# A three-phase float32 chain on one core: weight loads and splits moved between slots, a transposition done earlier, the third phase's first slot in another order

## The chip, the cores and the metric

One core of one Trainium2 chip runs the whole kernel. The metric is the device time of one execution in microseconds; before the change it was 1579.04 (median of 3 runs, 1578.59 to 1579.18).

## The reference

Inputs are float32, with batch 8, 8 heads, sequence 576, head size 64, so 4608 tokens of 512 features.

```python
kv = einsum('bhsd,bhse->bhde', k, v)
o  = einsum('bhsd,bhde->bhse', q, kv)
x  = o / sqrt(mean(o * o, -1) + 1e-6) * g_norm      # -> [4608, 512]
h  = x @ w_in                                        # [4608, 2048]
g  = (a0 + a1 h + a2 h^2 + a3 h^3) / (1 + |b0| |h| + |b1| h^2 + 1e-6)
x2 = g @ w_out                                       # [4608, 512]
e  = (x2 @ w1) * (x2 @ w2)                           # [4608, 1024]
out = (e @ w3) @ w_out2                              # [4608, 512]
```

The kernel gets the weights as float64 and makes float32 of them.

## The kernel before

Every product is made of three float32r matmuls: an operand is split into a rounded part `hi` (ScalarE) and the rest `lo` (VectorE), and `hi*hi`, `hi*lo` and `lo*hi` are summed in PSUM. The program is in manual order: each engine runs its instructions in the order in which the Python code issues them, and all transfers are issued by SyncE (SP) in that order. A tile is known by its tag; a new tile of a tag waits until the readers of the tile that it replaces are done. The names in the trace are those of the tiles.

**First phase** (to about 975 us): attention and the first pair of layers. Float64 weights are converted on the way.

**Second phase** (about 970 to 1332 us): `x2 @ w1` and `x2 @ w2`, combined in a seven-product scheme of Strassen's kind. `c_slot(n)` runs 48 times (6 groups of columns, `j`, times 8 feature blocks, `i`), and once more to drain; a slot holds seven products of six 128x384 matmuls each. In slot n TensorE does `a` and `c` of n, then `c` of n-1, `d` of n, `d` of n-1, and `b` and `a` of n. VectorE starts a slot by adding the carried sums to slot n-1's banks (L800 to L803), and products `c` and `d` of n-1 wait for that. Other work hangs on the slots in two lists: `extra1[n]` runs after the first two products, `extra2[n]` after slot n-1's `d`. The weights' pieces come in four sets of two feature blocks (`cw_load`, `cw_work`, the closures numbered 0 to 10); sets 0 and 1 are made on the boundary of the phases, set 2 in slots 2 and 3 and set 3 in slots 4 and 5, in runs of three or four closures. Slot 6 to 8 of each group make the next group's pieces of x (`gen_work`). `w_out2` (8 tiles, into the places `wa0` to `wa7`) is loaded in slots 44 and 45 (L882) and split in slots 46 and 47, four tiles at a time (`split_in`, L643 and L645). In slot 47 the first row of `w3` is loaded (`w3_load`, L866).

**Between the phases** the product `w3 @ w_out2` is built row block by row block, in the order `ROWS` = 0, 4, 1, 5, 2, 6, 3, 7. `w3_turn` transposes one row block of `w3` on TensorE (8 transposes, L874) and splits the result (L84, L85); the first turn stands ahead of the draining slot 48. `w_row(n)` does 24 matmuls 128x512 (L88 to L90) into one bank, and after its fifth k-step it turns the next row block. A row block lies in two tiles (tags `xh` and `xl`, two buffers each); the load for row n+2 is issued after row n. `w_out_row(n)` copies the bank out (L915) and makes the pieces `wq` of the third phase's weights. After each row two closures of `first_e` run: the sums and splits of the first 256 tokens of `e`.

**Third phase** (from 1387.81 us): `d_slot(n)`, 18 times and once to drain, again seven products, of twelve 128x256 matmuls each (L991), with the same waits between slots. `e_load(n)` loads 256 tokens of `e` in two halves of 512 KB into the tags that `R_SLOT` names (L952); for n = 1 the second half's tag is `wa7`, which holds a tile of `w_out2` until the last row is done. `e_work(n+1)`'s sums and splits run inside `d_slot(n)`: the lists `gen[0]` to `gen[2]`, two sums ahead of the first splits and two more between them.

Of the kernel before, what the change touches and what calls it, by code (L numbers as in the profile page):

```python
# [8 lines left out]
F32 = mybir.dt.float32  # L9
# [9 lines left out]
def linear_attention_two_moe_kernel(  # L19
# [24 lines left out]
    nc = tc.nc  # L44
# [362 lines left out]
    with tc.manual_schedule():  # L407
# [386 lines left out]
        def c_slot(n):  # L794
            cur = n if n < NGC else None
            e = cg.get(n - 1)
            if e:
                j_, i_ = divmod(n - 1, KF2)
                w_, q_ = cw[i_ // IP], pieces
                nc.vector.tensor_tensor(out=e["c"], in0=e["c"], in1=e["u"], op=ALU.add)  # L800
                e["c22"] = st_tile("c22")
                nc.vector.tensor_tensor(out=e["c22"], in0=e["c"], in1=e["p5"], op=ALU.add)
                nc.vector.tensor_tensor(out=e["d"], in0=e["d"], in1=e["u"], op=ALU.add)  # L803
                aS = st_tile("c11")
                nc.scalar.copy(aS, e["a"])
            if cur is not None:
                j, i = divmod(n, KF2)
                w, q = cw[i // IP], pieces
                f = cg[n] = {}
                names = ("at", "h", "h", "kv") if n % 2 == 0 else ("acc0", "acc1", "acc2", "acc3")  # L810
                for x, tag in zip("abcd", names):
                    f[x] = ps_tile(tag, [P, TA], 2 if tag == "h" else 1)
                prod(f["a"], w[A11], i, q[j, B11], True)
                nc.scalar.copy(f["b"], f["a"])
                prod(f["c"], w[S3], i, q[j, T3], True)
            for work in extra1.get(n, ()):
                work()
            if e:
                prod(e["c"], w_[A22], i_, q_[j_, T4], False)
                eo = wp.tile([P, 2, TA], F32, tag="wb15", name="eo")  # L820
                nc.vector.tensor_tensor(out=eo[:, 0, :], in0=aS, in1=e["c"], op=ALU.mult)
            if cur is not None:
                prod(f["d"], w[S1], i, q[j, T1], True)
                f["p5"] = st_tile("p5")
                nc.scalar.copy(f["p5"], f["d"])  # L825
            if e:
                prod(e["d"], w_[S4], i_, q_[j_, B22], False)
            for work in extra2.get(n, ()):
                work()
            if e:  # L830
                nc.vector.tensor_tensor(out=eo[:, 1, :], in0=e["c22"], in1=e["d"], op=ALU.mult)
                nc.sync.dma_start(
                    out=ed[i_, :, j_ * 2 * TA:(j_ + 1) * 2 * TA], in_=eo.rearrange("p a b -> p (a b)")
                )
                del cg[n - 1]
            if cur is not None:
                prod(f["b"], w[S2], i, q[j, T2], False)
                prod(f["a"], w[A12], i, q[j, B21], False)
                f["u"] = st_tile("u")
                nc.scalar.copy(f["u"], f["b"])  # L840

# [18 lines left out]

        def w3_load(i):
            for c in range(2):
                e = xp.tile([P, 3, W], F32R, tag=f"x{'hl'[c]}", name="w3")
                nc.sync.dma_start(out=f32(e[:, 2, :]), in_=w3d[i, :, c * W:(c + 1) * W])  # L866
                w3t[i, c] = e

        def w3_turn(i):
            for c in range(2):  # L870
                e = w3t[i, c]
                pt = ps_tile(("at", "kv")[c], [P, 4, P])
                for j in range(4):
                    nc.tensor.transpose(pt[:, j, :], f32(e[:, 2, j * P:(j + 1) * P]), ident)  # L874
                split(pt.rearrange("p j f -> p (j f)"), e[:, 0, :], e[:, 1, :])

        wo2 = {}
        wc = {}
# [7 lines left out]
        def w_row(n):  # L886
            i = ROWS[n]
            acc = ps_tile("h", [P, DM], bufs=2)
            for j in range(KF2):
                e = w3t[i, j // 4]  # L890
                sl = slice(j % 4 * P, (j % 4 + 1) * P)
                mm3(acc, e[:, 0, sl], e[:, 1, sl], *wo2[j], j == 0, j == KF2 - 1)
                if j == KF2 - 4 and n + 1 < KF2:
                    w3_turn(ROWS[n + 1])
            return acc

        NQ = DM // 2
        NPD = NT // (2 * P)  # L900
        KH = KF2 // 2
        wq = {}

        def wq_new(m):
# [7 lines left out]
        def w_out_row(n, acc):  # L912
            c, hf = n // 2, n % 2
            r = stp.tile([P, DM], F32, tag="st", name="wr")
            nc.scalar.copy(r, acc)  # L915
            wrow[hf] = r[:, :NQ], r[:, NQ:]

            def to(m, t):
                if m not in wq:
                    wq_new(m)  # L920
                split(t, *wq[m][c])

            if hf == 0:
                b11, b12 = wrow[0]
                to(B11, b11)
                sub(b11, b12, b11)
                to(T1, b11)
                return
            t1, b12 = wrow[0]
            b21, b22 = wrow[1]  # L930
            sub(b12, b22, b12)
            to(T3, b12)
            sub(t1, b22, t1)
            to(T2, t1)
            to(B21, b21)
            sub(t1, t1, b21)
            to(T4, t1)
            to(B22, b22)
# [7 lines left out]
        def e_load(n):  # L946
            if n >= NPD:
                return
            er[n] = []
            for h in range(2):  # L950
                t = wp.tile([P, KH, 2 * P], F32, tag=tags[R_SLOT[n % 2][h]], name="er")
                nc.sync.dma_start(  # L952
                    out=t, in_=ed[h * KH:(h + 1) * KH, :, n * 2 * P:(n + 1) * 2 * P].rearrange("k p t -> p k t")
                )
                er[n].append(t)

        def e_work(n):
            if n >= NPD:
                return [[], [], []]
            a11, a21 = er[n][0][:, :, :P], er[n][0][:, :, P:]  # L960
            a12, a22 = er[n][1][:, :, :P], er[n][1][:, :, P:]
            t = atp.tile([P, KH, P], F32, tag="kt", name="et", bufs=2)

            def to(m, x, sign=1.0):
                def f():
# [8 lines left out]
                        )  # L974
                return f

            return [
                [
                    lambda: nc.vector.tensor_tensor(out=t, in0=a21, in1=a22, op=ALU.add),
# [3 lines left out]
                [lambda: sub(t, a12, t), to(S4, t), to(A22, a22, -1.0)],  # L983
            ]

        def prod_d(bank, n, m, b, first):
            hi, lo = ex[n, m]
            for c in range(KH):
                wh, wl = wq[b][c]
                for x, (l, r) in enumerate(((hi, wh), (hi, wl), (lo, wh))):  # L990
                    nc.tensor.matmul(  # L991
                        bank, lhsT=l[:, c, :], rhs=r, start=first and c == 0 and x == 0,
                        stop=c == KH - 1 and x == 2, skip_group_check=True,
                    )
# [3 lines left out]
        def small(tag, name):  # L998
            return mp.tile([P, TA], F32, tag=tag, name=name, bufs=2)[:, :NQ]

        def d_slot(n):
            gen = e_work(n + 1)
            e = dg.pop(n - 1, None)
            f = None
# [7 lines left out]
            if n < NPD:  # L1012
# [3 lines left out]
                    f[x] = ps_tile(tag, [P, NQ], 2 if tag == "h" else 1)  # L1016
                prod_d(f["a"], n, A11, B11, True)
                nc.scalar.copy(f["b"], f["a"])
                prod_d(f["c"], n, S3, T3, True)
            for g in gen[0]:  # L1020
                g()
            r0 = (n - 1) * 2 * P
            if e:
                prod_d(e["c"], n - 1, A22, T4, False)
                nc.scalar.copy(o1[:, :NQ], e["c"])
                nc.sync.dma_start(out=out[r0 + P:r0 + 2 * P, :], in_=o1)
            if f:
                prod_d(f["d"], n, S1, T1, True)
                f["p5"] = small("a", "p5")
                nc.scalar.copy(f["p5"], f["d"])  # L1030
# [6 lines left out]
            for g in gen[2]:  # L1037
                g()
            if f:
                prod_d(f["b"], n, S2, T2, False)  # L1040
                prod_d(f["a"], n, A12, B21, False)
                f["u"] = small("y", "u")
                nc.scalar.copy(f["u"], f["b"])
            e_load(n + 3)
# [2 lines left out]
        CONV = "21011011120111120111110"  # L1047
        NG = NBA * MF
        LB = NG - MF
        extra1, extra2 = {}, {}  # L1050

        def add(d, n, *fs):
            d.setdefault(n, []).extend(fs)
# [128 lines left out]
        add(extra1, 1, u_upto(18), lambda: cw_load(2))  # L1182
        add(extra1, 2, u_upto(19))
        add(extra2, 2, lambda: cw_load(3))
        for n, ip in ((2, 2), (4, 3)):
            add(extra1, n, take(("cw", ip), 0, 1, 2, 3))
            add(extra2, n, take(("cw", ip), 4, 5, 6))
            add(extra1, n + 1, take(("cw", ip), 7, 8, 9, 10))
        for j in range(NPR):
            n0 = j * KF2  # L1190
            add(extra1, n0 + 3, lambda j=j: raw_x(j + 1))
# [11 lines left out]
                        add(extra2, n0 + c, lambda n=n: cv_load(n))  # L1203
        last = NGC - KF2
        for i in range(KF2):
            add(extra2, last + 4 + i // 4, lambda i=i: wo2_load(i))
            add(extra2, last + 6 + i // 4, lambda i=i: split_in(*wo2[i]))
        add(extra1, last + 7, lambda: w3_load(0))

        for g in range(NG + SK):  # L1210
            now[0] = g
# [37 lines left out]
            if g == NG:  # L1249
                c_slot(0)  # L1250
        for n in range(1, NGC + 1):
            if n == NGC:
                w3_turn(0)
            c_slot(n)
        w3_load(ROWS[1])
        e_load(0)
        first_e = [g for part in e_work(0) for g in part]
        for n in range(KF2):
            acc = w_row(n)
            if n + 2 < KF2:  # L1260
                w3_load(ROWS[n + 2])
            w_out_row(n, acc)
            for g in first_e[2 * n:2 * n + 2]:
                g()
        e_load(1)
        e_load(2)
        for n in range(NPD + 1):
            d_slot(n)
        mp_cm.__exit__(None, None, None)
        xp_cm.__exit__(None, None, None)  # L1270
# [34 lines left out]
```

## Time and profile before

| | before |
|---|---|
| median of 3 runs | 1579.04 us |
| the profiled execution | 1580.29 us |
| its span, first to last instruction | 1578.5 us |
| mean granted TensorE clock | 0.990 |
| TensorE busy | 1520.0 us, 96% |
| VectorE busy | 1245.5 us, 79% |
| ScalarE busy | 1056.5 us, 67% |
| GpSimd busy | 223.6 us, 14% |

The span lies 1.79 us below the time of the execution that was profiled, which itself was 1.25 us above the median of the three timed runs. Times within the trace count from the first instruction. A granted clock of 1.00 is 2.4 GHz, 0.50 is 1.2 GHz.

### The profile page before, as it was taken

The numbers are of one execution on the slowest core, as the hardware profiler recorded it, in microseconds if no ns is written. First come the engines' busy times: TensorE is split into PE (matmuls) and PEld (weight loads), VectorE is DVE, ScalarE is ACT, GpSimd is POOL, SyncE is SP. The second block draws the span as 40 slices with busy tenths as digits, with TensorE's granted clock in tenths as the row PEclk, the third lists the DMA queues.
The fourth block names the chain that finished last, engine by engine and source line by source line (L and its number), as shares of the span: only waits on it lengthen the run. The fifth ranks groups of instructions, "written<-read, shape, count | busy, mean of one in ns | idle before, by whom it ended". The sixth has DMA issues, their size and how long they took to land.

```text
span 1578.5 us, 26095 instructions
## 1 busy us (share of the span) xinstructions
PE 1520.0 (96%) x9640; PEld 1478.4 (94%) x9640; DVE 1245.5 (79%) x2373; ACT 1056.5 (67%) x2109; POOL 223.6 (14%) x201
## 2 busy tenths in 40 slices
PE   3699999999999999999999999999999998999999
PEld 3588999999999999999999999999999998789999
DVE  4899978778889888889898798867667664678885
ACT  3688877778888888888888887444344333555554
POOL 0122222212222222222222231000000000000000
PEclk9799999999999999999999999999999999999999
DMA  9846243431112111111111022253453444234552
GB/s 245 214 114 184 58 117 95 100 78 37 47 46 60 41 44 43 42 55 31 54 38 45 6 74 82 102 173 112 157 175 109 157 150 143 88 121 155 159 161 87
DMA packets 202079, 157.93 MB, mean 100 GB/s; under 512 B 122848, under 2 KB 179936, under 8 KB 201952
## 3 DMA queue, kind: packets, MB, share of 16 engines
q1 hardware_dynamic: 201952, 156.28, 33.3%
q8 instruction: 75, 1.23, 0.3%
q14 instruction: 52, 0.43, 0.1%
HBM read 106.43 MB, written 49.81 MB: 99 GB/s over the span
## 4 chain that ended last, share of the span: by engine, by line
PE 82%; DVE 10%; ACT 3%; DMA 2%; issue 1%; POOL 1%; SPq 1%; DVEq 0%; POOLq 0%; ACTq 0%
PE acc L783 11%; PE h L88 8%; PE h L90 8%; PE h L89 8%; PE acc L489 7%; PE acc L490 7%; PE acc L492 7%; PE acc L991 5%; PE h L783 5%; PE at L783 3%; PE kv L783 3%; PE h L991 2%; PE kv L991 2%; PE at L991 2%; PE at L350 1%
## 5 line engine op out<-in xcount | busy, mean ns | idle before, releaser
L539 POOL TENSOR_TENSOR s<-z,a 128x384 f32<-128x384 f32 x192 | 221.9, 1156 | 739.1 <-ACT z L536 659.0
L542 DVE TENSOR_TENSOR n<-n,h 128x384 f32<-128x384 f32 x192 | 105.5, 549 | 89.2 <-ACT n L537 87.5
L560 DVE SCALAR_TENSOR_TENSOR n<-n,na,y 128x384 f32<-128x384 f32 x192 | 157.7, 822 | 0.0
L535 ACT ACTIVATE a<-h 128x384 f32<-128x384 f32 x192 | 93.9, 489 | 95.3 <-PE h L90 94.4
L551 ACT ACTIVATE y<-s,epsq 128x384 f32<-128x384 f32 x192 | 118.3, 616 | 44.3 <-POOL s L539 43.2
L536 ACT ACTIVATE z<-a,ab 128x384 f32<-128x384 f32 x192 | 136.2, 709 | 6.4
L537 ACT ACTIVATE n<-h,na 128x384 f32<-128x384 f32 x192 | 125.5, 654 | 0.5 <-DVE lo L527 0.5
L544 DVE SCALAR_TENSOR_TENSOR n<-n,na,h 128x384 f32<-128x384 f32 x192 | 116.3, 606 | 0.5
L558 DVE SCALAR_TENSOR_TENSOR s<-s,y 128x384 f32<-128x384 f32 x192 | 107.6, 560 | 0.0
L527 DVE TENSOR_TENSOR lo<-n,hi 128x384 fp32r<-128x384 f32 x192 | 107.0, 557 | 0.0
L562 DVE SCALAR_TENSOR_TENSOR n<-s,n 128x384 f32<-128x384 f32 x192 | 105.4, 549 | 0.2
L552 ACT ACTIVATE y<-y 128x384 f32<-128x384 f32 x192 | 101.0, 526 | 6.1
L525 ACT CAST hi<-n 128x384 fp32r<-128x384 f32 x192 | 96.1, 500 | 1.3 <-DVE n L562 1.2
L269 PEld LDWEIGHTS kv<-vt,kt 128*64 128x64 f32 (+1 forms) x640 | 25.1, 153 | 26.5 <-issue 19.8
L269 PE MATMUL kv<-vt,kt 128*64 128x64 f32 (+1 forms) x640 | 30.9, 246 | 16.4 <-DMA vt<-in_v_dram 13.1
L825 ACT COPY p<-kv 128x384 f32<-128x384 f32 x24 | 11.5, 480 | 40.7 <-PE kv L783 29.4
L825 ACT COPY p<-acc 128x384 f32<-128x384 f32 x24 | 11.5, 480 | 40.3 <-PE acc L783 35.0
L350 PE MATMUL at<-kvbd,qT 128*128 128x128 f32 (+1 forms) x216 | 28.9, 284 | 5.5 <-DVE kvbd L288 3.7
L840 ACT COPY u<-acc 128x384 f32<-128x384 f32 x24 | 11.5, 479 | 33.6 <-PE acc L783 33.6
L350 PEld LDWEIGHTS at<-kvbd,qT 128*128 128x128 f32 (+1 forms) x216 | 26.4, 182 | 7.4 <-issue 4.0
L369 DVE TENSOR_REDUCE ms<-sq 128x8 f32<-128x512 f32 x36 | 24.5, 682 | 5.5 <-ACT sq L363 5.5
L800 DVE TENSOR_TENSOR acc<-acc,u 128x384 f32<-128x384 f32 x24 | 13.6, 566 | 19.0 <-ACT u L840 18.6
(1428 smaller groups left out, 4924.8 us busy)
## 6 DMA issues: line engine op xcount, KB each, us to landing
ed<-eo SPq DMA_DIRECT2D x48, 384.0 KB, 2.6
er<-ed SPq DMA_DIRECT2D x36, 512.0 KB, 3.9
x2d<-xev SPq DMA_DIRECT2D x48, 192.0 KB, 2.0
xr<-x2d SPq DMA_DIRECT2D x48, 192.0 KB, 4.0
out_dram<-o SPq DMA_DIRECT2D x36, 256.0 KB, 2.1
qt<-in_q_dram SPq DMA_DIRECT2D x32, 256.0 KB, 3.1
kt<-in_k_dram SPq DMA_DIRECT2D x32, 256.0 KB, 3.5
vt<-in_v_dram SPq DMA_DIRECT2D x32, 256.0 KB, 4.1
```

The source lines that it names most:

```text
L88: nc.tensor.matmul(outp, lhsT=lh, rhs=rh, start=first, stop=False)
L89: nc.tensor.matmul(outp, lhsT=lh, rhs=rl, start=False, stop=False)
L90: nc.tensor.matmul(outp, lhsT=ll, rhs=rh, start=False, stop=last)
L489: nc.tensor.matmul(accs[j][n], lhsT=wh[:, sl], rhs=e["hi"], start=first, stop=False)
L536: nc.scalar.activation(out=z, in_=a, func=AF.Identity, scale=ab[:, 1:2], bias=ab[:, 0:1])
L537: nc.scalar.activation(out=n, in_=h, func=AF.Identity, scale=na[:, 3:4], bias=na[:, 2:3])
L539: nc.gpsimd.tensor_tensor(out=s, in0=z, in1=a, op=ALU.mult)
L544: nc.vector.scalar_tensor_tensor(out=n, in0=n, scalar=na[:, 1:2], in1=h, op0=ALU.add, op1=ALU.mult)
L551: nc.scalar.activation(out=y, in_=e["s"], func=AF.Abs_reciprocal_sqrt, bias=epsq[:, 0:1])
L560: nc.vector.scalar_tensor_tensor(out=n, in0=n, scalar=na[:, 0:1], in1=y, op0=ALU.add, op1=ALU.mult)
L783: nc.tensor.matmul(bank, lhsT=lh[:, sl], rhs=x, start=first and kk == 0 and n == 0, stop=kk == 1 and n == 2, skip_group_check=True,)
L991: nc.tensor.matmul(bank, lhsT=l[:, c, :], rhs=r, start=first and c == 0 and x == 0, stop=c == KH - 1 and x == 2, skip_group_check=True,)
```

## The change

The change touches four places.

1. Sets 2 and 3 of the second phase's weight pieces: their closures no longer run in three runs of three or four, but in smaller runs from slot 2's `extra2` to slot 6's `extra1`.
2. A third list, `extra3[n]`, runs at the end of slot n. It loads `w_out2` two tiles per slot in slots 42 to 45; the tiles are split one in each of the two old lists in slots 44 to 47. `w3`'s first row is loaded at the end of slot 44 into tiles of the tags `vt` and `qt` and turned in slot 47's `extra2`, using PSUM tags `at` and `h`. The second row is loaded at the ends of slots 46 and 47, and `e_load(0)` follows. The first four k-steps of `w_row(0)` run in slot 48's `extra1`.
3. `w_row` turns the next row after its fourth k-step (after the sixth in row 0). The raw row block now lands in the `hi` part, so a tile has two planes in place of three. `e_load(1)` is issued after row 0: one half of 512 KB, and two quarters of 256 KB into the tags `vt` and `qt`. `first_e` has four closures more, `e_sums`, which make the sums of the second 256 tokens; the 15 closures are dealt out to the rows as 2, 1, 3, 1, 3, 1, 4, 0.
4. `d_slot(0)`: order `a`, `d`, then `c`, `b` and `a` over three of four k-steps, then the last k-step of these three. `w_out_row(7)` stops after its second piece, and the rest of it runs after `d`. `e_work(1)` holds splits alone.

```diff
@@ c_slot
                 nc.scalar.copy(f["u"], f["b"])
+            for work in extra3.get(n, ()):
+                work()
@@ w3_load, w3_turn, w_row
         def w3_load(i):
             for c in range(2):
-                e = xp.tile([P, 3, W], F32R, tag=f"x{'hl'[c]}", name="w3")
-                nc.sync.dma_start(out=f32(e[:, 2, :]), in_=w3d[i, :, c * W:(c + 1) * W])
-                w3t[i, c] = e
-
-        def w3_turn(i):
+                w3_half(i, c)
+
+        def w3_half(i, c):
+            if i == ROWS[0]:
+                hi, lo = (atp.tile([P, W], F32R, tag=("vt", "qt")[c], name="w3", bufs=2) for _ in range(2))
+            else:
+                e = xp.tile([P, 2, W], F32R, tag=f"x{'hl'[c]}", name="w3")
+                hi, lo = e[:, 0, :], e[:, 1, :]
+            nc.sync.dma_start(out=f32(hi), in_=w3d[i, :, c * W:(c + 1) * W])
+            w3t[i, c] = hi, lo
+
+        def w3_turn(i, tags=("at", "kv")):
...
-                if j == KF2 - 4 and n + 1 < KF2:
+                if j == (TURN if n else TURN0) and n + 1 < KF2:
                     w3_turn(ROWS[n + 1])
-            return acc
+                yield acc
...
+        TURN, TURN0, ROW0 = 3, 5, 4
@@ w_out_row
             to(T2, t1)
+            yield
             to(B21, b21)
@@ e_load, e_sums, e_work
-            for h in range(2):
+            for h in range(1 if n == 1 else 2):
...
+            if n == 1:
+                for c, tag in enumerate(("vt", "qt")):
+                    t = small_e(tag)
+                    nc.sync.dma_start(
+                        out=t, in_=ed[KH:, :, (n * 2 + c) * P:(n * 2 + c + 1) * P].rearrange("k p t -> p k t")
+                    )
+                    er[n].append(t)
...
+            def s1():
+                e1[1] = small_e("kt")
+                nc.vector.tensor_tensor(out=e1[1], in0=er[1][0][:, :, P:], in1=er[1][2], op=ALU.add)
+            def s2():
+                e1[2] = small_e("vt")
+                sub(e1[2], e1[1], er[1][0][:, :, :P])
+            def s3():
+                sub(er[1][0][:, :, P:], er[1][0][:, :, :P], er[1][0][:, :, P:])
+            def s4():
+                e1[4] = small_e("qt")
+                sub(e1[4], er[1][1], e1[2])
...
+            if n == 1:
+                return [
+                    [to(S3, a21), to(S1, e1[1])],
+                    [to(A11, a11), to(S2, e1[2]), to(A12, a12)],
+                    [to(S4, e1[4]), to(A22, a22, -1.0)],
+                ]
@@ d_slot
                 prod_d(f["a"], n, A11, B11, True)
                 nc.scalar.copy(f["b"], f["a"])
-                prod_d(f["c"], n, S3, T3, True)
+                if n == 0:
+                    prod_d(f["d"], n, S1, T1, True)
+                    f["p5"] = small("a", "p5")
+                    nc.scalar.copy(f["p5"], f["d"])
+                    run(out_row)
+                    prod_d(f["c"], n, S3, T3, True, range(KH - 1))
+                else:
+                    prod_d(f["c"], n, S3, T3, True)
             for g in gen[0]:
                 g()
...
-            if f:
+            if f and n == 0:
+                prod_d(f["b"], n, S2, T2, False, range(KH - 1))
+                prod_d(f["a"], n, A12, B21, False, range(KH - 1))
+            elif f:
                 prod_d(f["d"], n, S1, T1, True)
...
-                prod_d(f["b"], n, S2, T2, False)
-                prod_d(f["a"], n, A12, B21, False)
+                late = range(KH - 1 if n == 0 else 0, KH)
+                if n == 0:
+                    prod_d(f["c"], n, S3, T3, False, late)
+                prod_d(f["b"], n, S2, T2, False, late)
+                prod_d(f["a"], n, A12, B21, False, late)
@@ the lists
-        for n, ip in ((2, 2), (4, 3)):
-            add(extra1, n, take(("cw", ip), 0, 1, 2, 3))
-            add(extra2, n, take(("cw", ip), 4, 5, 6))
-            add(extra1, n + 1, take(("cw", ip), 7, 8, 9, 10))
+        for d, n, ip, ns in (
+            (extra2, 2, 2, (0, 1)), (extra1, 3, 2, (2, 3, 4)), (extra2, 3, 2, (9, 5, 6)), (extra1, 4, 2, (7, 8)),
+            (extra2, 4, 2, (10,)), (extra2, 4, 3, (0, 1)), (extra1, 5, 3, (2, 3, 4, 9)), (extra2, 5, 3, (5, 6, 7)),
+            (extra1, 6, 3, (8, 10)),
+        ):
+            add(d, n, take(("cw", ip), *ns))
...
-            add(extra2, last + 4 + i // 4, lambda i=i: wo2_load(i))
-            add(extra2, last + 6 + i // 4, lambda i=i: split_in(*wo2[i]))
-        add(extra1, last + 7, lambda: w3_load(0))
+            add(extra3, last + 2 + i // 2, lambda i=i: wo2_load(i))
+            add((extra1, extra2)[i % 2], last + 4 + i // 2, lambda i=i: split_in(*wo2[i]))
+        add(extra3, last + 4, lambda: w3_load(ROWS[0]))
+        add(extra3, last + 6, lambda: w3_half(ROWS[1], 0))
+        add(extra3, last + 7, lambda: w3_half(ROWS[1], 1), lambda: e_load(0))
+        add(extra2, last + 7, lambda: w3_turn(ROWS[0], ("at", "h")))
+        row0 = w_row(0)
...
+        add(extra1, last + 8, lambda: row_part(ROW0))
@@ main loops
         for n in range(1, NGC + 1):
-            if n == NGC:
-                w3_turn(0)
             c_slot(n)
-        w3_load(ROWS[1])
-        e_load(0)
-        first_e = [g for part in e_work(0) for g in part]
+        w3_load(ROWS[2])
+        first_e = [g for part in e_work(0) for g in part] + e_sums()
+        E_ROW = 2, 1, 3, 1, 3, 1, 4, 0
         for n in range(KF2):
-            acc = w_row(n)
-            if n + 2 < KF2:
+            for acc in row0 if n == 0 else w_row(n):
+                pass
+            if 0 < n and n + 2 < KF2:
                 w3_load(ROWS[n + 2])
-            w_out_row(n, acc)
-            for g in first_e[2 * n:2 * n + 2]:
+            out_row = w_out_row(n, acc)
+            next(out_row, None)
+            if n < KF2 - 1:
+                run(out_row)
+            if n == 0:
+                e_load(1)
+            for g in first_e[:E_ROW[n]]:
                 g()
-        e_load(1)
+            del first_e[:E_ROW[n]]
         e_load(2)
-        for n in range(NPD + 1):
+        d_slot(0, out_row)
+        for n in range(1, NPD + 1):
             d_slot(n)
```

## Rows read from the trace of the kernel before

**Rows 1.** The page's busy times and shares of the span.

```profile
PE 1520.0 (96%) x9640; PEld 1478.4 (94%) x9640; DVE 1245.5 (79%) x2373; ACT 1056.5 (67%) x2109; POOL 223.6 (14%) x201
```

**Rows 2.** Slots 3, 4, 6: length, PE, PEld, DVE, ACT, POOL, clock, DMA, GB/s.

```profile
990.46:999.81 9.35, 7.60 (x44) 7.31 (x43) 8.03 (x15) 4.92 (x10) 0.00 (x0) 1.00 0.59 188
999.81:1007.18 7.37, 7.37 (x43) 7.37 (x43) 6.17 (x11) 3.56 (x7) 0.00 (x0) 1.00 0.22 84
...
1014.55:1021.93 7.38, 7.38 (x44) 7.38 (x43) 6.37 (x14) 2.75 (x6) 0.00 (x0) 1.00 0.06 25
```

**Rows 3.** Same view: slot 47; slot 48, row 0; rows 1-7; two third-phase stretches.

```profile
1316.50:1324.04 7.54, 7.54 (x43) 7.28 (x43) 5.02 (x10) 3.88 (x8) 0.00 (x0) 1.00 0.38 125
1324.04:1342.55 18.51, 13.40 (x53) 11.02 (x52) 6.44 (x11) 2.73 (x5) 0.00 (x0) 0.82 0.43 142
1342.55:1387.81 45.26, 44.86 (x217) 36.26 (x216) 28.61 (x59) 22.54 (x49) 0.00 (x0) 1.00 0.23 76
1387.81:1409.16 21.35, 18.20 (x133) 17.53 (x132) 16.47 (x31) 11.54 (x26) 0.00 (x0) 0.92 0.44 136
1409.16:1419.24 10.08, 10.08 (x86) 10.08 (x85) 7.82 (x14) 5.86 (x13) 0.00 (x0) 1.00 0.50 158
```

**Rows 4.** TensorE's waits from 1320 to 1410: total us, times, longest.

```profile
PE acc L783 <- DVE c L802: 2.5, 1, 2.5
PE at L874 <- DMA w<-w3d: 2.1, 1, 2.1
PE acc L991 <- DVE o L1009: 1.9, 1, 1.9
PE at L991 <- DVE wa0hl L85: 0.6, 1, 0.6
PE acc L991 <- ACT acc L1018: 0.6, 1, 0.6
...
PE h L90 <- DVE w L85: 0.4, 2, 0.2
```

**Rows 5.** VectorE's timeline in slot 3.

```profile
992.72 0.55 DVE L831 TENSOR_TENSOR eo<-c,acc 128x384 f32<-128x384 f32 x1
...
993.77 0.56 DVE L802 TENSOR_TENSOR c<-h,p 128x384 f32<-128x384 f32 x1
```

**Rows 6.** TensorE's timeline: slot 48, and the starts of rows 1, 2 and 7.

```profile
1328.28 2.29 PE L783 MATMUL acc<-xq,wb7hl 128*128 128x384 f32 x6 [2.46 <-DVE c L802]
...
1342.55 0.40 PE L88 MATMUL h<-wa0hl,w 128*128 128x512 f32 x1
...
1349.00 0.39 PE L88 MATMUL h<-wa0hl,w 128*128 128x512 f32 x1
...
1382.22 0.39 PE L88 MATMUL h<-wa0hl,w 128*128 128x512 f32 x1
```

**Rows 7.** VectorE's timeline between slot 47 and slot 48.

```profile
1322.14 0.69 DVE L645 TENSOR_TENSOR wa4hl<-wa4hl 128x512 fp32r<-128x512 f32 x1 [1.30 <-ACT wa4hl L643]
...
1327.66 0.56 DVE L802 TENSOR_TENSOR c<-acc,p 128x384 f32<-128x384 f32 x1
```

**Rows 8.** Transfers issued in 1334.5 to 1337, then 1353 to 1376: count, KB, us to landing.

```profile
er<-ed SPq DMA_DIRECT2D x2, 512.0 KB, 7.2
w<-w3d SPq DMA_DIRECT2D x1, 256.0 KB, 7.7
...
w<-w3d SPq DMA_DIRECT2D x7, 256.0 KB, 2.7
```

**Rows 9.** The issuing queue's waits, 1340 to 1400.

```profile
SPq L952 <- PE h L90: 11.2, 1, 11.2
```

**Rows 10.** VectorE's timeline from the third phase's first sum to slot 0's carry.

```profile
1393.01 0.68 DVE L979 TENSOR_TENSOR et<-er 128x512 f32<-128x512 f32 x1
...
1400.27 0.68 DVE L972 SCALAR_TENSOR_TENSOR wa2hl<-er,wa2hl 128x512 fp32r<-128x512 f32 x1
...
1401.34 0.42 DVE L1009 TENSOR_TENSOR o<-acc,p 128x256 f32<-128x256 f32 x1
```

More of the change, by code (lines that the diff above doesn't have):

```diff
@@ L864, in w3_load @@
             for c in range(2):
-                e = xp.tile([P, 3, W], F32R, tag=f"x{'hl'[c]}", name="w3")
-                nc.sync.dma_start(out=f32(e[:, 2, :]), in_=w3d[i, :, c * W:(c + 1) * W])
-                w3t[i, c] = e
-        def w3_turn(i):
+                w3_half(i, c)
[8 more added lines that the diff above has]
+        def w3_turn(i, tags=("at", "kv")):
             for c in range(2):
-                e = w3t[i, c]
-                pt = ps_tile(("at", "kv")[c], [P, 4, P])
+                hi, lo = w3t[i, c]
+                pt = ps_tile(tags[c], [P, 4, P], 2 if tags[c] == "h" else 1)
                 for j in range(4):
-                    nc.tensor.transpose(pt[:, j, :], f32(e[:, 2, j * P:(j + 1) * P]), ident)
-                split(pt.rearrange("p j f -> p (j f)"), e[:, 0, :], e[:, 1, :])
+                    nc.tensor.transpose(pt[:, j, :], f32(hi[:, j * P:(j + 1) * P]), ident)
+                split(pt.rearrange("p j f -> p (j f)"), hi, lo)
         wo2 = {}
@@ L889, in w_row @@
             for j in range(KF2):
-                e = w3t[i, j // 4]
+                hi, lo = w3t[i, j // 4]
                 sl = slice(j % 4 * P, (j % 4 + 1) * P)
-                mm3(acc, e[:, 0, sl], e[:, 1, sl], *wo2[j], j == 0, j == KF2 - 1)
-                if j == KF2 - 4 and n + 1 < KF2:
+                mm3(acc, hi[:, sl], lo[:, sl], *wo2[j], j == 0, j == KF2 - 1)
+                if j == (TURN if n else TURN0) and n + 1 < KF2:
                     w3_turn(ROWS[n + 1])
-            return acc
+                yield acc
         NQ = DM // 2
@@ L955, in e_load, with small_e, e_sums @@
                 er[n].append(t)
+            if n == 1:
[5 more added lines that the diff above has]
+                    er[n].append(t)
+        def small_e(tag):
+            return atp.tile([P, KH, P], F32, tag=tag, name="et", bufs=2)
+        e1 = {}
+        def e_sums():
+            def s1():
[9 more added lines that the diff above has]
+                sub(e1[4], er[1][1], e1[2])
+            return [s1, s2, s3, s4]
         def e_work(n):
@@ L960, in e_work @@
             a11, a21 = er[n][0][:, :, :P], er[n][0][:, :, P:]
-            a12, a22 = er[n][1][:, :, :P], er[n][1][:, :, P:]
-            t = atp.tile([P, KH, P], F32, tag="kt", name="et", bufs=2)
+            if n == 1:
+                a12, a22 = er[n][1:]
+            else:
+                a12, a22 = er[n][1][:, :, :P], er[n][1][:, :, P:]
+                t = small_e("kt")
             def to(m, x, sign=1.0):
@@ L975, in to @@
                 return f
+            if n == 1:
+                return [
[3 more added lines that the diff above has]
+                ]
             return [
@@ L984, in e_work, with prod_d @@
             ]
-        def prod_d(bank, n, m, b, first):
+        def prod_d(bank, n, m, b, first, cs=range(4)):
             hi, lo = ex[n, m]
-            for c in range(KH):
+            for c in cs:
                 wh, wl = wq[b][c]
@@ L999, in small, with d_slot @@
             return mp.tile([P, TA], F32, tag=tag, name=name, bufs=2)[:, :NQ]
-        def d_slot(n):
+        def d_slot(n, out_row=()):
             gen = e_work(n + 1)
@@ L1018, in d_slot @@
                 nc.scalar.copy(f["b"], f["a"])
-                prod_d(f["c"], n, S3, T3, True)
+                if n == 0:
[4 more added lines that the diff above has]
+                    prod_d(f["c"], n, S3, T3, True, range(KH - 1))
+                else:
+                    prod_d(f["c"], n, S3, T3, True)
             for g in gen[0]:
@@ L1049, in linear_attention_two_moe_kernel @@
         LB = NG - MF
-        extra1, extra2 = {}, {}
+        extra1, extra2, extra3 = {}, {}, {}
         def add(d, n, *fs):
@@ L1205, in linear_attention_two_moe_kernel, with row_part @@
         for i in range(KF2):
-            add(extra2, last + 4 + i // 4, lambda i=i: wo2_load(i))
-            add(extra2, last + 6 + i // 4, lambda i=i: split_in(*wo2[i]))
-        add(extra1, last + 7, lambda: w3_load(0))
+            add(extra3, last + 2 + i // 2, lambda i=i: wo2_load(i))
[5 more added lines that the diff above has]
+        row0 = w_row(0)
+        def row_part(n):
+            for _ in range(n):
+                next(row0)
+        add(extra1, last + 8, lambda: row_part(ROW0))
         for g in range(NG + SK):
```

## Prediction

> **What bounds the kernel now.** I read the page first: TensorE is busy 1520.0 of 1578.5 us, VectorE 79%, ScalarE 67% [rows 1]. So only a stretch in which TensorE is idle or slow can give time, and the change touches two places. I cut these into stretches by the view of busy time and compared each with the work in it.
>
> A slot of the second phase without waits takes 7.37 us, 42 matmuls at 0.1755 us. Slot 3 takes 9.35 [rows 2]: 1.98 lost. Slot 47 takes 7.54 [rows 3]: 0.17 lost. From its end to row 0's end pass 18.51 us [rows 3]. The work in them: slot 48's twelve matmuls 2.11; a row without a turn 5.59 (row 7, from 1382.22 to the third phase's start at 1387.81); a turn 0.86 (row 1 has one and takes 6.45) [rows 3, 6]. With two turns that is 2.11 + 5.59 + 1.72 = 9.42, so 9.09 are lost. Rows 1 to 7 last 45.26; six rows of 6.45 and one of 5.59 are 44.29: 0.97 lost. The third phase's start, 1387.81 to 1409.16, holds eleven products of 10.08 / 7 = 1.44 us, 15.84 of 21.35 [rows 3]: 5.51 lost. All of it together, 17.72 us, is the most that the change can take away.
>
> Next I read the waits. In slot 48 and the turns TensorE waited 2.5 us for VectorE's sum L802 and 2.1 us for the load of w3's second row; in the third phase 1.9 us for L1009, and twice 0.6 us [rows 4]. Besides the idle time the granted clock is 0.82 over the 18.51 us and 0.92 over the 21.35 [rows 3]. The level is 1.2 GHz for a part of each, after these waits; 0.18 x 18.51 = 3.3 us and 0.08 x 21.35 = 1.7 us were lost by it. In slot 3 the clock stayed at 1.00 through its 1.75 us of idle time [rows 2]. So the long losses cost twice, once as a wait and once as slow matmuls behind it.
>
> **Second phase's start.** Slot 3's wait ends when L802 ends at 994.3, and that sum stood behind a backlog: VectorE was busy 8.03 us in this slot, and slot 2's last multiply, L831, ran at 992.72, in slot 3 already [rows 2, 5]. In slot 2 ran closures 0 to 6 of set 2, seven VectorE instructions; a split or a sum costs some 0.65 (0.68 and 0.69 long, overlapping by less than 0.1) [rows 7, 10]. Two of the seven stay there. Five leave, 3.2 us, more than the 1.98 to be gained. What comes later is slot 6: two splits are added to 6.37 us of VectorE, about 7.6 in a slot of 7.38 [rows 2]. Slot 7's L802 is due 2.11 us after the slot's start and needs 1.1 with the sum before it, so about 1.0 us of lag is free; 0.2 from slot 6 and some tenths from slot 5 fit. Bounds: the gain is 1.98, or the wait moves to slot 7 whole and it is 0. I take 1.8.
>
> **Slot 47 to row 0.** The loads of w_out2 move two to four slots ahead and hold eight transfers as before; their tiles `wa0` to `wa7` were last read in slots 42 and 43, so the queue stops for none. VectorE did four splits in slot 47 from 1322.14, then L831 and the two of the turn, and so L802 came at 1327.66, 3.6 us after slot 47's end at 1324.04 [rows 3, 7]. Now slot 47 has two w_out2 splits, at two places, and the turn inside it, with its 0.86 us of TensorE moved and not saved. I place L802 about 1 us after the slot's end, and four k-steps of row 0 (12 of 24 matmuls, 2.8 us) stand ahead of the product that needs it. That covers it by more than 1 us; without row 0's part it would be a wait of some tenths. The second row's load needs to land before the turn after six k-steps: it is issued about the end of slot 47 and due 2.8 + 2.1 + 1.4 = 6.3 us later. Such a load took 2.7 us alone and 7.7 behind 1 MB [rows 8]; `e_load(0)`'s 1 MB now stands behind it. I take 0 of wait, at most 1.4. With no wait nothing brings the clock down. So 9.09 + 0.17 come back, less a few tenths: I take 9.1, bounds 7.7 and 9.26.
>
> **Rows 1 to 7.** The two short waits (0.4 us idle) are for a split, L85, that was late because of two closures after an odd row [rows 4]. Odd rows now have one, 0.65 less. Even rows have two to four, but their chain is shorter by three pieces and two subtractions. Row 7 hides `e_sums`, four sums or 2.6 us, which have no turn beside them. The earlier turn has a price: the second tile of row n+2's load can be issued only when row n ends, and it is due four k-steps and half a turn later, 4 x 0.70 + 0.43 = 3.23 us, in place of 3.93. The seven loads issued in these rows took 2.7 us in the median [rows 8]; with 0.2 us from the row's end to the issue the margin is 0.3. I take 0.7 of the 0.97; bounds 0.97, and the third rival below.
>
> **Third phase's start.** `e_load(1)`'s second half stood 11.2 us in the queue until row 7's last matmul let `wa7` go [rows 9], and VectorE began its eleven instructions at 1393.01, 5.20 us after the row's end; the last ended at 1400.95, and then L1009 at 1401.76 let the waiting product go [rows 10]. Now the data are in and four of the eleven are done in row 7. The rest of row 7's pieces comes a little later (two copies of ScalarE go between), so seven splits start at about 6.0 and end at 6.0 + 7 x 0.61 = 10.3; with L1008 and L1009, 0.9 more, the product can go at about 11.25 after row 7's end. TensorE: slot 0's five products 7.2 without a wait, since the two first need nothing of row 7 and 2.88 us cover its pieces; slot 1's first product waits for the third of the seven splits, 7.9 instead of 7.45, 0.5; two products, 10.6; then 0.65 of wait. Of the 5.51 lost there stay 1.15, if the clock stays up, as it did through slot 3's longer wait: gain 4.3. If it falls as before, 1.7 less. I take 4.2; bounds 0.6 (the first wait alone [rows 4]) and 5.5.
>
> **Sum.** 1.8 + 9.1 + 0.7 + 4.2 = 15.8. The profiled execution took 1580.29 (span 1578.5 and 1.79 around it), so 1564.5; the median of the runs lay 1.25 below it, so 1563.2.
>
> **Rivals.** *The wait moves to slot 7.* VectorE is full in slots 5 to 7; the 1.8 is lost: 1565.0. Against it: the free 1.0 us. 1 in 10.
>
> *The third phase still starts late*, on the chain of splits: L802's counterpart waits on seven splits and TensorE slows behind it. Gain 0.6 in place of 4.2: 1566.8. For it: VectorE's order is one queue, and all seven stand before the sums. 14 in 100.
>
> *One load comes late.* `e_load(1)`, 1 MB, goes into the queue after row 0, ahead of the fourth row block's load. Behind 1 MB a load took 7.7 us [rows 8], so that turn would be 7.7 + 0.2 - 3.23 = 4.7 late: 1567.9. Against it: that load is first needed a whole row, 6.45 us, after `e_load(1)`'s issue. 8 in 100. The Trainium skill, page "DMA: Bandwidth & Descriptors", section "Queues, rings and completion order", says that each DMA engine consumes a queue's descriptors in ring order, so a small load stands behind a large one issued before it; by that rule this rival is the likelier the later `e_load(1)` goes. The trace agrees, with 7.7 us against 2.7 [rows 8].
>
> *Slower.* All five loads for rows 3 to 7 of the order, whose margin the earlier turn cut to 0.3, land as late as the crowded one: 5 x 4.7 = 23.5 lost, 1586.7. It decides from a landing of 3.03 + 15.8 / 5 = 6.2 us on. Against it: seven in these rows at a median of 2.7. 3 in 100.
>
> *No change.* The wait in slot 48 has another cause than the splits ahead of it, and returns at another place with the slow clock. 3 in 100.
>
> **Numbers.** My forecast has 62 in 100. A change below 0.2% (3.2 us) can't be told from none here. Faster takes the forecast and the first three rivals: 0.94; the same 0.03; slower 0.03. The low end is all 17.72 taken away, 1561.3, rounded down to 1561.0; the high end takes in the late load: 1568.0.
>
> **What would show it.** Slot 3 takes 7.4 us, with no wait for L802 there or in slot 7. From slot 47's end to row 0's end pass 8.6 us (the turn is in slot 47, which takes 8.2), at a clock of 1.00. The rows go at 6.45, and no turn waits for w3. From row 7's end to slot 2 pass 17 us, with waits below 0.7. I am wrong if a w3 load lands over 3.0 us after its issue, if slot 47's splits hold up L802 past row 0's part, or if TensorE's clock falls in the third phase.

## The result and the profile after

The changed kernel takes 1564.9 us (median of 4 runs, 1564.4 to 1565.16), the kernel before 1579.11 (4 runs, 1578.59 to 1581.56). The ratio is 0.9906, with a 95% interval of 0.9893 to 0.9919, so the change saves 14.2 us. The forecast was 1563.2, with a range of 1561.0 to 1568.0. The profiled execution took 1565.16 us, with a span of 1563.3.

The view of busy time by stretch, cut as in [rows 2, 3], shows slots 3, 4 and 6 first, then slot 7.

```profile
991.90:999.28 7.38, 7.38 (x44) 7.38 (x43) 5.64 (x10) 4.01 (x8) 0.00 (x0) 1.00 0.83 266
999.28:1006.65 7.37, 7.37 (x43) 7.37 (x43) 5.70 (x11) 3.49 (x7) 0.00 (x0) 1.00 0.13 53
...
1014.02:1021.40 7.38, 7.38 (x44) 7.38 (x43) 7.34 (x16) 3.79 (x8) 0.00 (x0) 1.00 0.13 53
1021.40:1028.77 7.37, 7.37 (x43) 7.25 (x43) 7.33 (x16) 4.40 (x10) 0.00 (x0) 1.00 0.14 56
```

Slot 3 is down from 9.35 to 7.38 us. VectorE (third pair) is now full in slots 6 and 7, 7.34 and 7.33 us, and the profile lists no wait of TensorE there. Slot 7 is a little longer all the same: slot 8 starts at 1028.83, 0.06 us behind the end of the last row shown. The same view for slot 47 with the turn in it, slot 48 with row 0, rows 1 to 7, and the third phase's start:

```profile
1316.03:1324.26 8.23, 8.23 (x52) 8.19 (x51) 4.92 (x10) 4.06 (x8) 0.00 (x0) 1.00 0.27 82
1324.26:1332.77 8.51, 8.51 (x45) 7.43 (x45) 3.67 (x8) 1.56 (x3) 0.00 (x0) 1.00 0.87 270
1332.77:1377.09 44.32, 44.32 (x217) 36.58 (x216) 31.47 (x64) 22.55 (x49) 0.00 (x0) 1.00 0.36 115
1377.09:1393.99 16.90, 16.35 (x133) 15.94 (x132) 13.52 (x26) 11.17 (x26) 0.00 (x0) 1.00 0.24 79
```

The first two take 16.74 us together, in place of 26.05, at a clock of 1.00. Rows 1 to 7 are down from 45.26 to 44.32, which is 0.03 above the work in them, and the third phase's start from 21.35 to 16.90. (The prediction speaks of "slot 2" as the end of this last stretch. It ends, before and after, where slot 1's last product starts, eleven products after row 7.) VectorE's sum L802, for which slot 48's first product waited before, and then all of TensorE's waits after 1300 us, which answer to [rows 4]:

```profile
1324.81 0.56 DVE L802 TENSOR_TENSOR c<-acc,p 128x384 f32<-128x384 f32 x1
```

```profile
PE acc L1041 <- DVE o L1059: 0.3, 1, 0.3
PE at L1041 <- DVE wa0hl L85: 0.2, 1, 0.2
```

L802 ends at 1325.37, 1.1 us after slot 47's end. All other waits are gone, and no turn waits for a load of w3. The loads themselves are not all fast. The view of transfers from 1300 to 1366 us, and then from 1335.8 to 1336:

```profile
w<-w3d SPq DMA_DIRECT2D x16, 256.0 KB, 3.0
w<-w3d SPq DMA_DIRECT2D x1, 256.0 KB, 4.6
```

Eight of the sixteen loads of w3 landed 3.3 to 4.6 us after their issue. The four places gave back 1.97 + 9.31 + 0.94 + 4.45 = 16.67 us between the two profiles. The two executions differ by 15.13, because slot 1 starts 1.45 us later in the second (976.60 against 975.15), before anything that changed; and the medians differ by 14.2. So the sum over the stretches is 2.5 us more than the medians give. The experiments had to find where these 2.5 us are, besides the worth of each part.

### The profile page after: what moved, and what is told of

Its sections match the earlier page's. It is cut to its first block, busy times and chain, and to the rows that moved or that the text cites. A ratio compares the mean times of both kernels' runs of the same rounds, so it can differ in the third digit from the quotient of the medians.

```text
span 1563.3 us, 26093 instructions
## 1 busy us (share of the span) xinstructions
PE 1514.7 (97%) x9640; PEld 1475.8 (94%) x9640; DVE 1245.2 (80%) x2373; ACT 1056.7 (68%) x2109; POOL 224.0 (14%) x201
## 3 DMA queue, kind: packets, MB, share of 16 engines
q8 instruction: 76, 1.25, 0.3%
## 4 chain that ended last, share of the span: by engine, by line
PE 85%; DVE 8%; ACT 2%; DMA 2%; issue 1%; POOL 1%; SPq 1%; DVEq 0%; POOLq 0%
PE acc L783 11%; PE h L88 9%; PE h L90 8%; PE h L89 8%; PE acc L489 7%; PE acc L490 7%; PE acc L492 7%; PE acc L1041 5%; PE h L783 5%; PE at L783 3%; PE kv L783 3%; PE h L1041 2%; PE kv L1041 2%; PE at L1041 2%; PE at L350 1%
## 5 line engine op out<-in xcount | busy, mean ns | idle before, releaser
L840 ACT COPY u<-h 128x384 f32<-128x384 f32 x24 | 11.5, 480 | 28.1 <-PE h L783 26.9
```

## The experiments

All numbers of stretches are read as above; the changed kernel's are 7.38 (slot 3), 16.74 (slot 47's start to row 0's end), 44.32 (rows 1 to 7) and 16.90 (row 7's end to slot 1's last product). An experiment has these too where nothing else is said, within 0.1. The time of an experiment is the median of its four runs, with their range behind it.

**Sets 2 and 3 in their old slots.**

```diff
-for d, n, ip, ns in (
...
-    add(d, n, take(("cw", ip), *ns))
+for n, ip in ((2, 2), (4, 3)):
+    add(extra1, n, take(("cw", ip), 0, 1, 2, 3))
+    add(extra2, n, take(("cw", ip), 4, 5, 6))
+    add(extra1, n + 1, take(("cw", ip), 7, 8, 9, 10))
```

> The changed kernel with sets 2 and 3 of the second phase's weight pieces made in their old slots. My theory: the wait in slot 3 is VectorE's backlog alone and adds up with nothing else, so slot 3 goes from 7.38 us back to 9.35, slots 6 and 7 stay at 7.4, every other stretch stays as it is, and the time rises by 2.0 us. Rival: the wait had another cause (the loads of the pieces, which did not move), slot 3 stays at 7.4 and the time within 0.3 us.

Slot 3 took 9.35 us again, slots 6 and 7 7.37, and the time was 1566.87 (1565.38 to 1567.36). The theory holds: this place is worth 1.97 us, or 1.91 with slot 7's 0.06 taken off, and it adds to the rest.

**The splits of w_out2 in their old slots.**

```diff
-add((extra1, extra2)[i % 2], last + 4 + i // 2, lambda i=i: split_in(*wo2[i]))
+add(extra2, last + 6 + i // 4, lambda i=i: split_in(*wo2[i]))
```

> The changed kernel with the eight splits of w_out2 back in the second list of slots 46 and 47, four at a time; loads, turn and row 0's part stay new. My theory: two splits more in slot 47 put VectorE's sum L802 1.2 us later, to 2.3 us after the slot's end, and row 0's four k-steps (2.8 us) still cover it: the stretch from slot 47's start to row 0's end goes from 16.74 us to 16.7 to 17.1. Rival: the clump was the cause of the long wait by itself, and the stretch grows by 1 us or more.

The stretch from slot 47's start to row 0's end takes 16.93 us, and the time is 1564.12 (1563.21 to 1564.63). VectorE's timeline shows the first of four splits that stand in one run again, and L802 behind them:

```profile
1320.31 0.69 DVE L645 TENSOR_TENSOR wa4hl<-wa4hl 128x512 fp32r<-128x512 f32 x1 [1.35 <-ACT wa4hl L643]
...
1324.98 0.56 DVE L802 TENSOR_TENSOR c<-acc,p 128x384 f32<-128x384 f32 x1
```

Slot 47 takes 8.4 us here, 0.2 more. It ends at 1323.1 and L802 at 1325.5, 2.5 us later, which row 0's part (2.8 us) just covers. So with that part in place the spreading of the splits is worth about 0.2 us, no more. What it is worth without that part was not run.

**No part of row 0 ahead of slot 48's products.**

```diff
-TURN, TURN0, ROW0 = 3, 5, 4
+TURN, TURN0, ROW0 = 3, 5, 0
```

> The changed kernel without the four k-steps of row 0 ahead of slot 48's products; the whole row comes behind them. My theory: L802 ended 1.1 us after slot 47's end, so slot 48's first product waits about 1.2 us, the clock stays at 1.00 as it did after slot 3's 1.75 us in the kernel before, and the stretch from slot 47's start to row 0's end is 17.9 us. Rival 1: the wait is hidden and the stretch stays at 16.7. Rival 2: the clock falls behind the wait and the stretch is 19 us or more.

The stretch takes 17.97 us, with one wait of 1.00 us for L802 and no fall of the clock:

```profile
1323.54 1.31 PE L783 MATMUL acc<-xq,wb7hl 128*128 128x384 f32 x6 [1.00 <-DVE c L802]
```

Rows 1 to 7 took 44.40, and the time is 1565.16 (1564.51 to 1566.14). The theory holds.

**The turn behind slot 47, and no part of row 0.**

```diff
-TURN, TURN0, ROW0 = 3, 5, 4
+TURN, TURN0, ROW0 = 3, 5, 0
...
-add(extra2, last + 7, lambda: w3_turn(ROWS[0], ("at", "h")))
...
+            if n == NGC:
+                w3_turn(ROWS[0], ("at", "h"))
             c_slot(n)
```

> The changed kernel with the first turn of w3 back between slots 47 and 48 and without row 0's part ahead of slot 48; the loads and the spread splits stay new. My theory: the turn's two splits stand ahead of L802 on VectorE, their chain (transposes 0.86, ScalarE, two splits, two sums) makes slot 48's first product wait some 2.5 us, and the clock falls behind it as before, for 1.5 to 3 us more: the stretch from slot 47's start to row 0's end is 20.5 to 22.5 us. Rival: the spread splits alone had removed the wait, and the stretch stays below 18 us.

The stretch takes 19.61 us, which is below the range that I gave. The wait is as long as in the kernel before, and the clock does not fall. TensorE's timeline,

```profile
1325.24 1.32 PE L783 MATMUL acc<-xq,wb7hl 128*128 128x384 f32 x6 [2.63 <-DVE c L802]
1326.40 1.22 PE L783 MATMUL acc<-xq,wb11hl 128*128 128x384 f32 x6
```

shows 1.32 us for the first six matmuls behind the wait, where the kernel before shows 2.29 behind 2.46 us [rows 6]. So the clock's part of the theory failed for this execution. This run undoes two things, and the run before it one of them: the place of the turn is worth 19.61 - 17.97 = 1.64 us, and row 0's part 17.97 - 16.74 = 1.23. The four times were 1566.03, 1566.14 (the profiled one), 1569.04 and 1569.39. The upper two may have had a slow clock behind the wait; they have no trace, and the mean clocks on record for the four, 0.993, 0.993, 0.996 and 0.991, do not settle it.

**The old order in the third phase's slot 0,** with `e_load(1)` and its sums still early: `a`, `c`, `d`, `b`, `a` whole, and row 7's pieces in one run.

```diff
-                if n == 0:
-                    prod_d(f["d"], n, S1, T1, True)
...
-                    run(out_row)
-                    prod_d(f["c"], n, S3, T3, True, range(KH - 1))
-                else:
-                    prod_d(f["c"], n, S3, T3, True)
+                prod_d(f["c"], n, S3, T3, True)
...
```

> The changed kernel with the old order in the third phase's slot 0 and row 7's pieces in one run, but with the second 256 tokens of e still loaded and summed early. My theory: slot 0 waits 0.8 us again for ScalarE's copy, but the seven splits then start about 0.6 us earlier and slot 1 has no wait, so from row 7's end to slot 2 pass 16.6 to 17.0 us where the changed kernel has 16.90: the order by itself is worth nothing. Rival: the order is worth the wait it removes, and the stretch is 17.7 us or more.

The stretch from row 7's end takes 16.77 us, with one wait of 0.66 for ScalarE's copy and none in slot 1; the time is 1564.85 (1563.64 to 1565.42). The new order removes a wait of 0.7 us in slot 0 and makes two waits, 0.2 and 0.3, in slot 1. With the early load it is worth nothing.

**The second 256 tokens of e behind row 7 again.**

```diff
-for h in range(1 if n == 1 else 2):
+for h in range(2):
...
-        first_e = [g for part in e_work(0) for g in part] + e_sums()
-        E_ROW = 2, 1, 3, 1, 3, 1, 4, 0
+        first_e = [g for part in e_work(0) for g in part]
+        E_ROW = 2, 1, 3, 1, 3, 1, 0, 0
...
-            if n == 0:
-                e_load(1)
...
+        e_load(1)
         e_load(2)
```

> The changed kernel with the second 256 tokens of e loaded behind row 7 again, into a place that a tile of w_out2 held, and its four sums made inside slot 0; the new order of slot 0 stays. My theory: this load and its sums are the third phase's loss. VectorE then ends its eleven instructions some 3.5 us later, slot 1's third product waits about 4 us, and the clock falls behind it, so the stretch from row 7's end to slot 2 goes from 16.90 us to 20.5 to 22.5. Rival: the new order covers the late load and the stretch stays below 18.5 us.

The view by stretch, from row 7's end to slot 1's last product:

```profile
1375.32:1395.72 20.40, 18.09 (x133) 17.45 (x132) 16.26 (x30) 11.57 (x26) 0.00 (x0) 0.92 0.44 143
```

The stretch takes 20.40 us, at a clock of 0.92, and the time is 1568.28 (1566.86 to 1570.11). The waits come at other places than I expected: 1.0 and 0.9 us in slot 1's first product, and 0.4 in the third, since the second product runs slowly and hides the rest. The size is 0.1 below my range. So the early load is worth 3.50 of the 4.45 us, with a fall of the clock in it: 0.08 x 20.40 = 1.6 us, by estimate. The order is not quite without worth where the load is late. This run has the new order and the late load, and is 0.95 us shorter than the kernel before (21.35), at the same mean clock of 0.92.

**The next row turned after the third k-step.**

```diff
-TURN, TURN0, ROW0 = 3, 5, 4
+TURN, TURN0, ROW0 = 2, 5, 4
```

> The changed kernel with the next row block turned after the third k-step in place of the fourth, in rows 1 to 6. My theory: the second half of a row block is issued 0.2 us after the row before ends and lands 2.6 to 2.7 us later, so it is 0.3 to 0.4 us late for a turn that is due at 3 x 0.70 + 0.43 = 2.53 us; in the five rows 2 to 6 this gives 1.5 to 2.0 us, so rows 1 to 7 take 45.9 to 46.3 us where the changed kernel takes 44.32. Rival: the loads have more slack than I work out and the rows stay at 44.3.

Rows 1 to 7 took 46.40 us, 0.1 above my range, with five waits for the load, one in each row that I named. The time is 1565.87 (1564.99 to 1566.04).

```profile
PE kv L883 <- DMA w<-w3d: 1.1, 5, 0.3
```

The loads landed 2.6 us after their issue. The turn came one k-step, 0.70 us, earlier, and each of the five rows lost 0.42, of which 0.22 was idle. So the turn after the fourth k-step stands some 0.3 to 0.5 us from the edge.

**The rows as before.**

```diff
-TURN, TURN0, ROW0 = 3, 5, 4
+TURN, TURN0, ROW0 = 4, 5, 4
...
-E_ROW = 2, 1, 3, 1, 3, 1, 4, 0
+E_ROW = 2, 2, 2, 2, 2, 2, 3, 0
```

> The changed kernel with the rows as before: the next row block turned after the fifth k-step, and two closures of e after nearly every row. My theory: the two closures after rows 1, 3 and 5 make the next row's split late, so two or three waits of 0.3 to 0.5 us come back and rows 1 to 7 take 45.0 to 45.6 us, where the changed kernel takes 44.32. Rival: the waits came from the late turn's load and not from VectorE's closures, and the rows stay at 44.3 to 44.5.

Rows 1 to 7 took 45.76 us, somewhat above my range, with three waits for a split (L85), in rows 3, 5 and 7, whose splits stand behind the closures after rows 1, 3 and 5. The time is 1565.29 (1564.64 to 1565.64). The wait in row 3:

```profile
1345.67 0.50 PE L90 MATMUL h<-wa0hl,w 128*128 128x512 f32 x1 [0.20 <-DVE w L85]
```

A wait of 0.2 us idle costs its row 0.47: the rows take 6.92 against 6.45. Without a wait these matmuls last 0.40 us and start 0.23 us apart, so a wait takes their overlap of 0.17 too, and the matmul behind it takes 0.10 more. The run undoes the earlier turn and the dealing out of the closures together, so it does not say what each is worth.

**A load right behind 1 MB.**

```diff
-            if 0 < n and n + 2 < KF2:
+            if n == 1:
+                w3_half(ROWS[3], 1)
+                e_load(1)
+                w3_half(ROWS[3], 0)
+            elif 0 < n and n + 2 < KF2:
                 w3_load(ROWS[n + 2])
...
-            if n == 0:
-                e_load(1)
```

> The changed kernel with the 1 MB of e for the second 256 tokens issued after row 1 in place of row 0, and the first half of the fourth row block issued right behind it. My theory, that of the late load: a 256 KB load behind 1 MB lands some 5 to 7.7 us after its issue, which is about 1.5 us after row 1's end, so the turn in row 2, due 2.8 us after it, waits 4 to 6 us, and rows 1 to 7 take 48 to 51 us with the clock falling behind the wait. Rival: the transfers share the engines, the load lands in 3 to 4.5 us, and rows 1 to 7 take 46 to 47.5 us.

Rows 1 to 7 took 51.35 us, a little above the range, and the time was 1571.58 (1571.4 to 1572.23). The load, TensorE's timeline at the turn of row 2, and the view by stretch behind it:

```profile
w<-w3d SPq DMA_DIRECT2D x1, 256.0 KB, 6.1
```

```profile
1347.13 1.08 PE L883 MATMUL at<-ident,w 128*128 128x128 f32 x4 [5.43 <-DMA w<-w3d]
```

```profile
1347.13:1352.90 5.77, 5.77 (x23) 4.98 (x24) 1.38 (x2) 1.65 (x3) 0.00 (x0) 0.74 0.01 3
```

The load landed 6.1 us after its issue, the turn waits 5.43 us, and the row takes 13.49 in place of 6.46. The clock of 0.74 behind the wait is about the other 1.6. So the rival of the late load was real in its mechanism, and dearer than the 4.7 us that the prediction gave it: 7.0, because the clock fell too. In the changed kernel the last piece of `e_load(1)` is issued at 1333.55 us and the next load of w3 at 1335.76. That load landed in 4.6 us, at 1340.34, and its turn was due at 1342.04. So 1.7 us of room kept the rival out, and not a whole row.

**The third phase's splits in the order of need.**

```diff
+                late1.extend([to(S4, e1[4]), to(A22, a22, -1.0)])
                 return [
-                    [to(S3, a21), to(S1, e1[1])],
-                    [to(A11, a11), to(S2, e1[2]), to(A12, a12)],
-                    [to(S4, e1[4]), to(A22, a22, -1.0)],
+                    [to(A11, a11), to(S3, a21)],
+                    [to(S1, e1[1]), to(S2, e1[2]), to(A12, a12)],
+                    [],
                 ]
...
-            for g in gen[0]:
+            for g in (late1 if n == 1 else []) + gen[0]:
                 g()
```

> A version that may beat both: the changed kernel with the splits for the third phase's slot 1 begun with the piece that its first product needs, and with the two pieces that only slot 2 needs split inside slot 1, behind the carried sums. My theory: slot 1's two waits (0.24 and 0.31 us idle) go, so from row 7's end to slot 2 pass 15.9 us where the changed kernel has 16.90, and the time falls by 1.0 us, with no new wait in slot 2. Rival: the two splits moved into slot 1 make slot 2's first piece late, and the stretch to slot 3 gets no shorter.

The stretch takes 15.84 us, which is eleven products and nothing else; TensorE has no wait that the view lists from 1300 to 1560 us. The time is 1563.22 (1563.11 to 1564.33), and the ratio to the kernel before is 0.9899 (0.9884 to 0.9913). In the trace it is shorter than the changed kernel by the 1.06 us that were left. The medians differ by as much (1564.37 below), but that alone would not show it: the run with the splits in their old slots gained nothing in its stretches and has a median of 1564.12.

**The changed kernel once more.**

> The changed kernel once more, as it is. In its profile the first phase ended 1.45 us later than in that of the kernel before, with the same code up to there. My theory: this is the spread of the loads in the first 60 us from one execution to the next, so the start of slot 1 moves by 0.5 to 2 us between these profiles, and the time by as much. Rival: the change itself makes the first phase longer, and slot 1 starts at 976.6 us again.

Slot 1 starts at 975.79 us, 0.8 earlier than in the first profile, and the four stretches repeat within 0.03. In all fourteen profiles, with the same code up to there, slot 1 starts between 974.72 and 976.60. The 1.45 us are this spread, and not the change's. The time is 1564.37 (1564.25 to 1564.45), and the ratio 0.9905 (0.989 to 0.992).

**The kernel before once more.**

> The kernel before once more, as it is. Between the two profiles the changed stretches gave back 16.7 us, between the medians 14.2. My theory: what the clock costs after a wait is not the same in every execution, so in a second profile of the kernel before the two long stretches (26.05 us from slot 47's start to row 0's end, 21.35 us from row 7's end on) differ from the first by 1 us or more, while the waits themselves are equal within 0.1 us. Rival: both stretches repeat within 0.3 us, and only the first phase, slot 1's start at 975.15 us, moves, by up to 2 us.

The stretch from slot 47's start to row 0's end took 25.75 us, 0.3 less, most of it a shorter wait for the load (1.85 us in place of 2.07). The other took 19.85, 1.50 less. The view by stretch, and TensorE's timeline behind the same wait:

```profile
1387.38:1407.23 19.85, 16.70 (x134) 16.03 (x132) 16.17 (x30) 11.55 (x26) 0.00 (x0) 1.00 0.46 147
```

```profile
1401.38 1.69 PE L991 MATMUL acc<-wq,wb8hl 128*128 128x256 f32 x12 [1.86 <-DVE o L1009]
1402.91 1.60 PE L991 MATMUL kv<-wq,wa3hl 128*128 128x256 f32 x12
```

The wait is equal to 0.01 us, and no slow clock follows: 1.00 in place of 0.92 [rows 3]. The theory holds for this stretch. The other moved by 0.3 us only, as the rival had it, and the clock fell in it both times. Against this profile the four places give back 1.98 + 9.01 + 0.97 + 2.96 = 14.9 us (second profiles of both kernels), near the medians' 14.2.

## Why the prediction was right

The faster case came, by the mechanisms named, and the time lies 1.7 us above the forecast, inside the range. The gain was put at 15.8 us and came to 14.2.

*Second phase's start:* taken at 1.8, measured 1.97. The fear for slot 7 was hardly borne out, although VectorE is full there: it lost 0.06.

*Slot 47 to row 0:* taken at 9.1, measured 9.31 and 9.01. L802 ended 1.1 us after slot 47's end, as placed. The experiments price the parts: the turn inside slot 47 (1.64) and row 0's part (1.23) cover the sum and are worth 2.9 us together, with no fall of the clock; the spreading of the splits, which I described as the relief of VectorE, 0.2. The larger remainder, 26.05 - 19.61 = 6.4 us, was not undone by itself. In the kernel before it answers to the wait for the second row's load, 2.1, a wait of 0.5 inside the first turn, and the slow clock, some 3.3 by the prediction's estimate, 5.9 together. That these are its cause is read from the two traces, where they are gone after the change; no run brings them back one by one.

*Rows:* taken at 0.7, measured 0.94 and 0.97. The margin of 0.3 us that I worked out for the earlier turn is borne out from its far side, by the turn one k-step earlier. One sign that I named for being wrong did appear, a w3 load that lands over 3.0 us after its issue: eight of sixteen did. The sign was drawn too wide. The limit of 3.0 holds for the second tiles of the last five row blocks alone, and these landed in 2.6 to 2.7 us; the others were issued earlier against their turns, and none held TensorE up.

*Third phase's start:* taken at 4.2. This is the term that was mis-sized. It held 1.7 us for the slow clock behind the last wait, read from one execution as if every execution paid it. The first profile gives 4.45, the second 2.96. Within it I had the parts right in sum and not in share: the reordering of slot 0, to which I gave the first wait, is worth nothing beside the early load, because what it takes from slot 0 it puts into slot 1; the early load of e is worth 3.5, with a fall of the clock in that run. Some 0.4 us of the excess is offset by the second phase and the rows, which were taken 0.2 and 0.2 to 0.3 too small.

*The median:* I took 1.25 us off the profiled execution's sum, as if it stood outside the stretches. The changed kernel's profile lies 0.26 above its median. Most of the 1.25 can be the same slow clock, 1.5 us in one of two profiles; that the timed runs divide in this way was not seen, as they have no trace.

The page "DMA: Bandwidth & Descriptors" of the Trainium skill, section "Queues, rings and completion order", says that each DMA engine consumes a queue's descriptors in ring order. The run that put a load behind 1 MB agrees: it landed 6.1 us after its issue, against 2.6 for the loads that went alone.

## What to carry to other kernels

A chain on VectorE that ends late can be hidden by independent matmuls put ahead of the product that waits, without thinning out the chain: four k-steps of row 0 covered the sum with the splits in either place. A small load that is soon due is not put right behind a large one: right behind 1 MB it cost 7.0 us, and 2.2 us later it cost nothing. Where a stretch has lost time to a fall of the clock, its price is read from two profiles before it goes into a sum.

## What the runs showed of the hardware

In these traces the granted clock does not follow the length of a wait alone. Behind a wait of 1.86 to 1.87 us at the same place of the same program it fell in one execution of the kernel before (0.92 over the stretch) and stayed at 1.00 in another; behind 2.63 us (the turn behind slot 47) it stayed at 1.00, behind 2.46 and 2.47 us (slot 48 of the kernel before, twice) it fell. The kernel before ran from 1577.93 to 1581.56 over all its runs, the changed one from 1564.25 to 1565.16 over its eight. That the clock makes this difference is not shown: with sets 2 and 3 in their old slots the times went from 1565.38 to 1567.36, and in that run's profile the clock stayed at 1.00 through the second and third phases.
